# Top-k attention with an MLP behind it: 25 more items transposed by VectorE and DRAM, and q and k loaded in fewer DMAs

## The chip, the cores and the metric

The kernel runs on one core of one Trainium2 chip. The time is that of the device in microseconds (us), median of the runs of one kernel. A profile is one further execution with the hardware profiler. Engines are named as the profile names them: PE (TensorE), DVE (VectorE), ACT (ScalarE), POOL (GpSimd), SP (SyncE, which here only issues DMAs).

## What is computed

```python
scores = scale * np.matmul(q, k.transpose(0, 1, 3, 2))        # q, k, v: (8, 8, 576, 64) f32
kth = np.partition(scores, -32, axis=-1)[..., -32:-31]
scores = np.where(scores >= kth, scores, -1e9)
attn = np.exp(scores - max); attn = attn / (attn.sum(-1) + 1e-9)
x = np.matmul(attn, v)                                         # then (B, S, H*D) = 4608 x 512
g = gelu_exact(x @ w_in)                                       # w_in: 512 x 2048
out = g @ w_out                                                # w_out: 2048 x 512
```

All of it is float32. Each row of 576 scores keeps its 32 largest, and the softmax is taken over these.

## The kernel before

**Items.** Two heads make a pair (32 pairs in all, four to a batch). An item is one tile of 128 query rows of a pair, with both heads side by side: a tile of 128 x 1152 scores (`S_of`, tag "s", six buffers, L378). 576 rows are four tiles of 128 and 64 rows over; the 64 rows of two pairs form an item of their own. There are 18 items to a batch and 144 in all; `items` (L247 to L254) lists them so that tile t = 0 and 1 of pair 0 come first, then of pairs 1 to 3, then t = 2 and 3. In even batches the two items of the 64 rows stand last, in odd ones first. Thus an even item has t even, the odd one after it is the next tile of the same pair, and the two share one product with v.

**Slots.** The loop at L1154 runs over slots n. In slot n the scores of items ahead are made (L375; in even slots those of n+2 and n+3, the first in a PSUM tile of tag l1, which the MLP's first layer also uses, the second in tag pr), DVE does the top-k of item n (`top_k`, L457: four rounds of MAX8 and MATCH_REPLACE8 on each half), ACT does the selection and the exponentials of item n-1 (L512, L522), DVE takes the reciprocal of its sums at the end of the top-k (L504), POOL multiplies the item by it (`normalise`, L552). Item n-2 is transposed, so that keys lie on the partitions, and item n-3, if odd, is multiplied by v with the even one before it (`attend`, L696): ten products o of 128 x 64 and 128 x 256, and ACT copies o to xT (L720). The bank of o, of the transposes of the tails, of the last 64 keys' scores (L349) and of the first product of the second layer ("seven", L927) is one and the same, tag z.

**Two ways to transpose.** Most items go over PE: nine transposes against the identity (L619, L649) into PSUM, and two copies by ACT (L629, L664) into the tile `pt` (L597, L610; one buffer). Items for which `squared` (L558) holds, 48 even ones from item 28 on, go another way: in the middle of the top-k of slot i+2, ahead of its third round, DVE transposes squares of 32 x 32 (`square_p`, L565, one instruction over 128 x 1152), SP writes them to DRAM in four DMAs after that slot's top-k (`write_p`, L571), and at the start of slot i+3 reads them back into `pt` in four DMAs (`read_p`, L581), where the squares come to lie as a full transpose. An even item's `pt` is used in slot i+4.

**q and k.** From the second batch on, k and q of a pair are loaded in squares (L118 to L128) and turned by DVE (L282 to L288); the rows 512 to 575 of the two heads go to places of their own. Their loads are issued by SP when the pair before has been transposed (L314 to L317). v is loaded by tiles (L129 to L134).

**The MLP.** Its matmuls are cut in pieces (`l1_piece` L764, `trio_piece` L954, `seven_piece` L938), which `mlp` (L1077) puts between the attention's work so that each slot has its share: an even slot has seven pieces of the first layer, the odd slot after it the eighth, then "seven" and six of the second layer. Every engine, and SP's queue, works in the order in which this program issues.

Of the kernel before, what the change touches and what calls it, by code (L numbers as in the profile page):

```python
# [14 lines left out]
def kernel(  # L15
# [19 lines left out]
    nc = tc.nc  # L35
# [6 lines left out]
    P = 128  # L42
# [68 lines left out]
    def load(n, pair, queue=None, queue2=None):  # L111
        if pair >= n_pairs:
            return
        queue = queue or nc.sync
        queue2 = queue2 or queue
        b, h0 = pair // NP, 2 * (pair % NP)
        src = sources[n]
        if n != "v" and pair >= SQUARES:  # L118
            t = flat[n][0]
            for e in range(2):  # L120
                for d in range(2):
                    rows, cols = slice((2 * e + d) * SQ, (2 * e + d + 1) * SQ), slice(d * SQ, (d + 1) * SQ)
                    for at, lo, hi, by in ((0, 0, SM, queue), (SM + e * TL, SM, S, queue2)):
                        by.dma_start(
                            out=t[rows, at : at + hi - lo].rearrange("i (c j) -> i c j", j=SQ),
                            in_=src[b, h0 + e, lo:hi, cols].rearrange("(c i) j -> i c j", i=SQ),
                        )
            return  # L128
        t = raw_of(n, pair)  # L129
        for e in range(2):  # L130
            queue.dma_start(
                out=t[:, 0:NM, e, :], in_=src[b, h0 + e, 0:SM].rearrange("(t p) d -> p t d", p=P)
            )
            queue2.dma_start(out=t[e * TL : (e + 1) * TL, NM, e, :], in_=src[b, h0 + e, SM:S])  # L134

    load("k", 0, nc.scalar, nc.gpsimd)
    load("q", 0)
# [138 lines left out]
    def transpose_qk(pair, first=False):  # L276

        q_tail = SM + P
        done = set()

        def squares(c):
            rq, rk, kt = flat["q"][0], flat["k"][0], kt_of.get(pair)  # L282
            if c == 0:
                nc.vector.transpose(kt[:, 0:q_tail], rk)
            elif c == 1:
                nc.vector.transpose(kt[:, q_tail:], rq[:, SM:])
# [35 lines left out]

    S_of, stat_of = {}, {}

    def row(i, e):
        return S_of[i][:, e * S : (e + 1) * S]

# [16 lines left out]
    def last_keys(i, t_ps):  # L344
# [3 lines left out]
        if t < NM:  # L348
            nc.tensor.matmul(  # L349
                t_ps[:, 0:P], lhsT=q_of[pair][:, t * P : (t + 1) * P],  # L350
                rhs=kt_of[pair][:, SM : SM + P], start=True, stop=True,
            )
            if i == 0:
                return lambda: nc.vector.tensor_scalar(
                    s[:, SM : S + TL], t_ps[:, 0:P], scale, None, op0=ALU.mult
                )
            return lambda: nc.scalar.activation(
                s[:, SM : S + TL], t_ps[:, 0:P], func=AF.Copy, scale=scale
            )
        for r in range(2):  # L360
            kt = kt_of[pair + r]
            for e in range(2):
                nc.tensor.matmul(
                    t_ps[half(r, e), r * TL : (r + 1) * TL],
                    lhsT=kt[:, SM + P + e * TL : SM + P + (e + 1) * TL],
                    rhs=kt[:, SM + e * TL : SM + (e + 1) * TL],
                    start=True, stop=True,
                )
        return lambda: nc.scalar.activation(
# [4 lines left out]
    def scores(i, second=False):  # L374
# [7 lines left out]
        if t < NM:  # L382
            q_t, kt = q_of[pair][:, t * P : (t + 1) * P], kt_of[pair]
            for e in range(2):
                rows = slice(e * D, (e + 1) * D)
                nc.tensor.matmul(  # L386
                    s_ps[:, e], lhsT=q_t[rows, :], rhs=kt[rows, 0:SM], start=True, stop=True
                )
            if i == 0:

# [4 lines left out]
        else:  # L395

            for r in range(2):
                kt = kt_of[pair + r]
                for e in range(2):
                    rows = slice(e * D, (e + 1) * D)  # L400
                    nc.tensor.matmul(
                        s_ps[half(r, e), r, :], lhsT=kt[rows, SM + P + e * TL : SM + P + (e + 1) * TL],
                        rhs=kt[rows, 0:SM], start=True, stop=True,
                    )
            s2 = s.rearrange("p (r n) -> p r n", r=2)
            nc.scalar.activation(s2[:, :, 0:SM], s_ps, func=AF.Copy, scale=scale)
# [164 lines left out]
    def write_p(i):  # L571

        if squared(i):
# [3 lines left out]
            for a in range(P // SQ):  # L577
                rows = slice(a * SQ, (a + 1) * SQ)
                nc.sync.dma_start(out=d[:, :, rows], in_=s[rows])

    def read_p(i):  # L581

        if squared(i):
            d = turned.pop(i)
            for k in range(P // SQ):
                nc.sync.dma_start(
                    out=pt_now[0][k * SQ : (k + 1) * SQ, :, 0:P], in_=d[:, :, k, :]
                )

    def transposes(i):  # L590
# [3 lines left out]
        if squared(i):  # L594

            def keys_only(ahead):
                pt_now[0] = work.tile([P, 2 * NM + 1, 2 * P], f32, tag="pt", bufs=1, name="pt")  # L597
                if ahead is not None and ahead < N:
                    last_keys(ahead, bank("t_ps"))()

# [4 lines left out]
        def tails(ahead):  # L605
# [1 line left out]
            keys = last_keys(ahead, tp) if ahead is not None and ahead < N else None  # L607
            at = P
            if t % 2 == 0:
                pt_now[0] = work.tile([P, 2 * NM + 1, 2 * P], f32, tag="pt", bufs=1, name="pt")  # L610
            if diag is not None:
                for e in range(2):
                    nc.tensor.matmul(
# [540 lines left out]
    for n in range(ahead):  # L1154
# [165 lines left out]
```

## Time and profile before

| | |
|---|---|
| time, median of 3 runs (lowest to highest) | 1480.86 us (1480.14 to 1481.07) |
| the profiled execution | 1479.73 us, its span 1478.0 us |
| busy over the span: ACT, POOL | 74%, 77% |
| granted PE clock | 1.0 all through |
| DMA: moved, mean rate | 112.94 MB, 76 GB/s |

A span is from the first to the last instruction of the profiled execution. A row of a timeline has start and duration in us, engine, line, operation, tiles and shapes, how many instructions it merges, and in brackets the idle time ahead of them with what ended it. Matrix products and PE's float32 work come as two instructions each, transposes as one.

### The profile page before, as it was taken

What the parts mean: (1) busy time and instruction counts of PE and PEld (TensorE: products, weight loads), DVE (VectorE), ACT (ScalarE), POOL (GpSimd) and SP (SyncE); (2) the same over time, 40 slices, a digit from 0 to 9 for tenths busy, and PEclk for the clock granted to TensorE, in tenths of its full rate; (3) what the DMA queues carried; (4) which work ended last, traced back from release to release, by engine and by line L of the source; (5) the groups of instructions that cost most, each with busy time, mean ns of one, the idle gap of its engine ahead of it and who ended that gap; (6) DMA issues with size and microseconds to landing.
All of it is one profiled execution on the core that took longest, in us unless ns stands there. A gap on an engine that the chain in (4) does not pass through costs nothing. (4 is left out here: it accounts for less than half of the span.)

```text
span 1478.0 us, 27006 instructions
## 1 busy us (share of the span) xinstructions
PE 1461.6 (99%) x8817; PEld 1147.9 (78%) x8817; DVE 1294.3 (88%) x3318; ACT 1099.9 (74%) x1942; POOL 1140.1 (77%) x1291
## 2 busy tenths in 40 slices
PE   8999999999999999999999999999999999999999
PEld 6876677877777777887777778787777777787787
DVE  8999899999999988999999987999999997998701
ACT  7999977877777687777777778777777777776620
POOL 6877567877898879877898978886788887987732
PEclk9999999999999999999999999999999999999999
DMA  7424310045435322345534331345453421233300
GB/s 198 143 86 124 84 48 1 24 88 101 95 73 93 66 58 52 65 95 108 105 83 81 69 61 47 66 93 99 97 103 73 89 55 41 61 61 72 70 15 15
DMA packets 477645, 112.94 MB, mean 76 GB/s; under 512 B 413216, under 2 KB 469056, under 8 KB 477504
## 3 DMA queue, kind: packets, MB, share of 16 engines
q1 hardware_dynamic: 476240, 110.78, 35.3%
q8 instruction: 70, 1.15, 0.3%
q14 instruction: 71, 0.58, 0.1%
q10 hardware_dynamic: 1200, 0.39, 0.1%
q0 software_dynamic: 64, 0.03, 0.0%
HBM read 73.39 MB, written 37.75 MB: 75 GB/s over the span
## 5 line engine op out<-in xcount | busy, mean ns | idle before, releaser
L773 PE MATMUL h_ps<-xT,w_in_sb 128*128 128x256 f32 (+1 forms) x2560 | 536.2, 361 | 0.1
L773 PEld LDWEIGHTS h_ps<-xT,w_in_sb 128*128 128x128 f32 x2560 | 436.5, 190 | 73.4 <-issue 25.2
L483 DVE MAX8 top<-lists 128x8 f32<-128x576 f32 (+1 forms) x792 | 476.4, 641 | 0.0
L486 DVE MATCH_REPLACE8 lists<-top,lists 128x288 f32<-128x288 f32 (+1 forms) x528 | 307.9, 589 | 0.0
L552 POOL TENSOR_TENSOR s<-s,rden 128x1152 f32<-128x1152 f32 x135 | 285.8, 2117 | 0.3 <-DVE rden L504 0.3
L529 ACT ACTIVATE s<-s,bias 128x576 f32<-128x576 f32 x288 | 225.4, 787 | 11.0 <-issue 0.4
L517 ACT ACTIVATE s<-s,neg 128x576 f32<-128x576 f32 x288 | 225.5, 793 | 1.7 <-POOL neg L497 1.6
L510 POOL TENSOR_SCALAR den<-den 128x2 f32<-128x2 f32 x144 | 31.4, 218 | 215.9 <-ACT s L529 210.2
L455 POOL TENSOR_TENSOR lists<-lists 128x576 int32<-128x576 int32 x132 | 186.2, 1410 | 4.0
L447 POOL TENSOR_TENSOR lists<-s 128x576 int32<-128x576 int32 x133 | 187.2, 1407 | 0.0
L715 PE MATMUL o<-pt,raw_v 128*64 128x256 f32 x1280 | 153.0, 384 | 1.8 <-ACT s L529 1.1
L715 PEld LDWEIGHTS o<-pt,raw_v 128*64 128x64 f32 x1280 | 87.8, 136 | 85.8 <-issue 37.2
L789 ACT ACTIVATE g<-h_ps 128x512 f32<-128x512 f32 x144 | 78.2, 594 | 100.6 <-PE h_ps L773 100.4
L929 PE MATMUL y_ps<-w_out_sb,sum 128*128 128x256 f32 x472 | 140.4, 379 | 0.0
L394 ACT ACTIVATE s<-s_ps 128x1024 f32<-128x1024 f32 x127 | 125.5, 1035 | 10.5 <-PE s_ps L386 10.3
L664 ACT COPY pt<-tp 128x1024 f32<-128x1024 f32 x85 | 86.6, 1019 | 62.2 <-PE tp L649 62.1
L386 PE MATMUL s_ps<-kt,qm 64*128 64x512 f32 x512 | 129.4, 618 | 0.8 <-ACT s L392 0.8
L504 DVE RECIPROCAL rden<-den 128x2 f32<-128x2 f32 x144 | 23.2, 161 | 108.6 <-POOL den L510 107.4
L486 DVE MATCH_REPLACE8 lists<-first,lists 128x288 f32<-128x288 f32 x264 | 114.3, 439 | 0.0
L929 PE MATMUL y_ps<-w_out_sb,g 128*128 128x256 f32 x480 | 113.4, 379 | 0.0
L483 DVE MAX8 first<-lists 128x8 f32<-128x288 f32 x268 | 106.6, 436 | 0.0
L929 PEld LDWEIGHTS y_ps<-w_out_sb,g 128*128 128x128 f32 x480 | 91.2, 190 | 12.4
(167 smaller groups left out, 2533.1 us busy)
## 6 DMA issues: line engine op xcount, KB each, us to landing
turned<-s SPq DMA_DIRECT2D x192, 144.0 KB, 3.5
pt<-turned SPq DMA_DIRECT2D x192, 144.0 KB, 3.2
raw_v<-in_v_dram SPq DMA_DIRECT2D x64, 128.0 KB, 2.4
out_dram<-y SPq DMA_DIRECT2D x30, 256.0 KB, 2.1
raw_q<-in_q_dram SPq DMA_DIRECT2D x112, 64.0 KB, 2.0
raw_k<-in_k_dram SPq DMA_DIRECT2D x112, 64.0 KB, 2.0
w_out_sb<-in_moe_w_in_dram SPq DMA_DIRECT2D x14, 511.8 KB, 4.8
w_out_sb<-in_moe_w_out_dram SPq DMA_DIRECT2D x10, 511.8 KB, 4.1
```

What stands on the lines that cost most here:

```text
L386: nc.tensor.matmul(s_ps[:, e], lhsT=q_t[rows, :], rhs=kt[rows, 0:SM], start=True, stop=True)
L394: nc.scalar.activation(spread(s, S + TL, SM), s_ps, func=AF.Copy, scale=scale)
L447: nc.gpsimd.tensor_tensor(t[:, :, 1].bitcast(i32), a.bitcast(i32), b.bitcast(i32), op=ALU.add)
L455: nc.gpsimd.tensor_tensor(into_of(i)[:, :, 1].bitcast(i32), both, top, op=ALU.subtract)
L483: nc.vector.max(x[:, e], src[:, e])
L486: nc.vector.match_replace(dst[:, e], x[:, e], src[:, e], LOWEST)
L517: nc.scalar.activation(s, s, func=AF.Prelu, bias=st["neg"][:, e : e + 1], scale=1.0, alpha=STEEP)
L529: nc.scalar.activation(s, s, func=AF.Exp, bias=st["bias"][:, e : e + 1], scale=1.0, accum_out=st["den"][:, e : e + 1],)
L552: nc.gpsimd.tensor_tensor(s, s, wide, op=ALU.mult)
L715: nc.tensor.matmul(o[e * D : (e + 1) * D, 0:n], lhsT=vt[:, j, e, :], rhs=pt[:, e * NJ + j if j < NM else NM, :], start=(j == 0), stop=(j = ...
L773: nc.tensor.matmul(h_tile(u)[:, i, :], lhsT=w_in_sb[:, ko, f * P : (f + 1) * P], rhs=xT[:, ko, c0 : c0 + n], start=(ko == 0), stop=(ko == ...
L929: nc.tensor.matmul(acc[names][:, k], lhsT=lhsT, rhs=rhs, start=(j == 0 and k == 0), stop=(j == FT // 2 - 1 and k == 1),)
```

## The change

`squared` now also holds for an odd item whose pair is even within its batch and which is followed by an item that goes by squares (or by an item of the 64 rows). These are 25: 29, 33, 37, 41, 45, 49; 57 to 85 in steps of 4; 93 to 121 in steps of 4; 129, 133 and 137. Their tile is transposed by DVE in slot i+2, written at its end and read at the start of slot i+3, into the odd half of `pt`; `later` holds for them, and their product with v (with the copy of o) is issued at the end of slot i+3 and not after its scores. `pt` is now allocated where the even half is read.

The loads of k and q in squares take all 576 rows of a head and half in one DMA, four DMAs in place of eight. Both heads' keys lie in one run of 576 columns, the second head's 64 columns further on; the 64 keys that are handled apart are the first ones of the first head and the last ones of the second, so the columns of the main keys are 64 to 575 and the matmul of the last keys reads two runs of 64 columns, 576 apart (`both_ends`). The rows of v of the first head are taken in the matching order, and q's tail is 64 columns wide instead of 128 for DVE's transpose. The corner of k's tile that has to be zero is set once in slot 5.

```diff
@@ load
-                    for at, lo, hi, by in ((0, 0, SM, queue), (SM + e * TL, SM, S, queue2)):
-                        by.dma_start(
-                            out=t[rows, at : at + hi - lo].rearrange("i (c j) -> i c j", j=SQ),
-                            in_=src[b, h0 + e, lo:hi, cols].rearrange("(c i) j -> i c j", i=SQ),
-                        )
+                    queue.dma_start(
+                        out=t[rows, at : at + S].rearrange("i (c j) -> i c j", j=SQ),
+                        in_=src[b, h0 + e, :, cols].rearrange("(c i) j -> i c j", i=SQ),
+                    )
...
+            end = TL if pair >= SQUARES and e == 0 else S
+            main = end % S
@@ squares
-                nc.vector.transpose(kt[:, q_tail:], rq[:, SM:])
+                nc.vector.transpose(kt[:, q_tail : q_tail + TL], rq[:, SM:S])
@@ last_keys
-                rhs=kt_of[pair][:, SM : SM + P], start=True, stop=True,
+                rhs=both_ends(pair), start=True, stop=True,
@@ squared
-        return SINGLE.stop - 2 < i < N - 2 and i % 2 == 0 and items[i][1] < NM and i % RINGS != 12
+        if not SINGLE.stop - 2 < i < N - 2 or items[i][1] == NM:
+            return False
+        if i % 2 == 0:
+            return i % RINGS != 12
+        return items[i][0] % 2 == 0 and (squared(i + 1) or items[i + 1][1] == NM)
+
+    def later(i):
+
+        return i % 2 == 1 and squared(i)
@@ read_p
             d = turned.pop(i)
+            if i % 2 == 0:
+                pt_now[0] = pt_tile()
             for k in range(P // SQ):
                 nc.sync.dma_start(
-                    out=pt_now[0][k * SQ : (k + 1) * SQ, :, 0:P], in_=d[:, :, k, :]
+                    out=pt_now[0][k * SQ : (k + 1) * SQ, :, i % 2 * P : (i % 2 + 1) * P], in_=d[:, :, k, :]
                 )
@@ the loop over slots
-        product = attend(n - 3)
+        product = not later(n - 3) and attend(n - 3)
...
         run_gelus()
         mlp(left[0])
         run_gelus()
+        if later(n - 3):
+            attend(n - 3)
+            copy_x()
         if n < N:
             top_k(n, lambda: inverse(n - 1), lambda: square_p(n - 2))
             write_p(n - 2)
@@ n == 5
+            nc.vector.memset(flat["k"][0][TL:, 0:TL], 0.0)
```

More of the change, by code (lines that the diff above doesn't have):

```diff
@@ L323, with main_keys, end_keys, both_ends @@
     S_of, stat_of = {}, {}
+    def main_keys(pair):
+        return slice(TL, TL + SM) if pair >= SQUARES else slice(0, SM)
+    def end_keys(pair, e):
+        at = e * (SM + TL) if pair >= SQUARES else SM + e * TL
+        return slice(at, at + TL)
+    def both_ends(pair):
+        kt = kt_of[pair]
+        return spread(kt, SM + TL, TL) if pair >= SQUARES else kt[:, SM : SM + P]
+    def end_rows(pair, e):
+        at = SM + P + (0 if pair >= SQUARES else e * TL)
+        return slice(at, at + TL)
     def row(i, e):
@@ L364, in last_keys @@
                     t_ps[half(r, e), r * TL : (r + 1) * TL],
-                    lhsT=kt[:, SM + P + e * TL : SM + P + (e + 1) * TL],
-                    rhs=kt[:, SM + e * TL : SM + (e + 1) * TL],
+                    lhsT=kt[:, end_rows(pair + r, e)], rhs=kt[:, end_keys(pair + r, e)],
                     start=True, stop=True,
@@ L386, in scores @@
                 nc.tensor.matmul(
-                    s_ps[:, e], lhsT=q_t[rows, :], rhs=kt[rows, 0:SM], start=True, stop=True
+                    s_ps[:, e], lhsT=q_t[rows, :], rhs=kt[rows, main_keys(pair)], start=True, stop=True
                 )
@@ L401, in scores @@
                     nc.tensor.matmul(
-                        s_ps[half(r, e), r, :], lhsT=kt[rows, SM + P + e * TL : SM + P + (e + 1) * TL],
-                        rhs=kt[rows, 0:SM], start=True, stop=True,
+                        s_ps[half(r, e), r, :], lhsT=kt[rows, end_rows(pair + r, e)],
+                        rhs=kt[rows, main_keys(pair + r)], start=True, stop=True,
                     )
@@ L579, in write_p, with pt_tile @@
                 nc.sync.dma_start(out=d[:, :, rows], in_=s[rows])
+    def pt_tile():
+        return work.tile([P, 2 * NM + 1, 2 * P], f32, tag="pt", bufs=1, name="pt")
     def read_p(i):
@@ L596, in keys_only @@
             def keys_only(ahead):
-                pt_now[0] = work.tile([P, 2 * NM + 1, 2 * P], f32, tag="pt", bufs=1, name="pt")
                 if ahead is not None and ahead < N:
@@ L609, in tails @@
             if t % 2 == 0:
-                pt_now[0] = work.tile([P, 2 * NM + 1, 2 * P], f32, tag="pt", bufs=1, name="pt")
+                pt_now[0] = pt_tile()
             if diag is not None:
```

5 lines of the change are left out of this document (3 added, 2 removed).

## The prediction

> **What bounds the kernel now.** I read the page first, then the waits, then the timeline of TensorE, ScalarE, VectorE and SyncE over a few slots in the middle.
>
> ```profile
> span 1478.0 us, 27006 instructions
> PE 1461.6 (99%) x8817; PEld 1147.9 (78%) x8817; DVE 1294.3 (88%) x3318; ACT 1099.9 (74%) x1942; POOL 1140.1 (77%) x1291
> ```
>
> ```profile
> DVE rden L504 <- POOL den L510: 107.4, 92, 9.7
> ```
>
> TensorE has next to no idle time, so it sets the pace. VectorE is close behind: nearly all of its idle time (107.4 us over 92 of the 144 items) is a wait at the reciprocal that ends each top-k, for the sum that ScalarE delivers. The two therefore run in step, and a part moved from one to the other counts twice. The profiled execution took 1479.73 us (span plus 1.7), 1.1 below the median of the runs, so I add what I work out to the median, 1480.86.
>
> The timeline of TensorE (start, duration, instruction, count) around the product of item 69, one of the 25, and the transposes of item 71, which is not:
>
> ```profile
> 700.74 1.99 PE L386 MATMUL s_ps<-kt,qm 64*128 64x512 f32 x8
> 702.66 2.38 PE L715 MATMUL o<-pt,raw_v 128*64 128x256 f32 x20
> 704.97 2.86 PE L773 MATMUL h_ps<-xT,w_in_sb 128*128 128x256 f32 x12
> 707.66 0.38 PE L349 MATMUL t_ps<-kt,qm 128*128 128x128 f32 x2
> 707.88 4.48 PE L773 MATMUL h_ps<-xT,w_in_sb 128*128 128x256 f32 x20
> 712.20 1.03 PE L927 MATMUL seven<-w_sum,g 128*128 128x256 f32 x4
> ...
> 715.87 0.27 PE L619 MATMUL tp_t<-ident,s 128*128 128x128 f32 x1
> 715.98 0.60 PE L929 MATMUL y_ps<-w_sum,sum 128*128 128x256 f32 x2
> ...
> 716.85 1.04 PE L649 MATMUL tp<-ident,s 128*128 128x128 f32 x8
> 717.72 0.60 PE L929 MATMUL y_ps<-w_sum,g 128*128 128x256 f32 x2
> ```
>
> The starts follow each other without a gap, so the distance to the next start is what an instruction costs the path: 2.31 us for the product (702.66 to 704.97), 0.86 for a first-layer piece (a fifth of 707.88 to 712.20), 0.98 for the transposes of an item (0.11 at L619, 0.87 at L649).
>
> **The change, part by part.** Transposes taken off TensorE: 25 x 0.98 = 24.5 us. ScalarE loses the copies L629 and L664 with them, which is no gain by itself.
>
> VectorE gets 25 transposes. What one costs, where the even items have theirs:
>
> ```profile
> 578.75 0.14 DVE L504 RECIPROCAL rden<-den 128x2 f32<-128x2 f32 x1
> ...
> 582.69 1.41 DVE L483 MAX8 top<-lists 128x8 f32<-128x576 f32 x2
> ...
> 587.00 0.17 DVE L504 RECIPROCAL rden<-den 128x2 f32<-128x2 f32 x1
> ...
> 590.92 1.36 DVE L569 STREAM_TRANSPOSE s<-s 128x1152 f32<-128x1152 f32 x1
> 592.21 1.37 DVE L483 MAX8 top<-lists 128x8 f32<-128x576 f32 x2
> ...
> 596.60 0.17 DVE L504 RECIPROCAL rden<-den 128x2 f32<-128x2 f32 x1 [0.24 <-POOL den L510]
> ```
>
> 1.29 us each (590.92 to 592.21), 32 in all, against 107.4 of idle time: it fits on the whole, with little to spare where the items lie. In a slot without a transpose the third round starts 3.94 us after the reciprocal before it (578.75 to 582.69): there item 57's would go.
>
> The product moves behind the seven first-layer pieces that its slot has. Before, it stood between the scores and these pieces. The scores' first tile has the tag l1, as h_ps has, and ScalarE empties it:
>
> ```profile
> 701.98 1.94 ACT L394 ACTIVATE s<-s_ps 128x1024 f32<-128x1024 f32 x2 [0.27 <-PE s_ps L386]
> ```
>
> The first of the two copies ends at 702.95, the scores on TensorE at 702.66. With the product gone from between, the first piece waits 0.3 us and a hand-over, 0.35, in the 22 of 25 slots with two score items. Behind the moved product the eighth piece (0.86 us) covers the copy of o before the bank z is needed again: nothing. By TensorE alone that leaves 24.5 - 7.7 = 16.8 us gained.
>
> **The new wait** is the round trip through DRAM. An even item has two slots for it; an odd one is transposed in one slot and multiplied in the next. The SyncE queue, and what its transfers take to land:
>
> ```profile
> 592.35 3.26 SPq L579 DMA_DIRECT2D turned<-s  x4
> 598.47 2.54 SPq L586 DMA_DIRECT2D pt<-turned  x4
> ```
>
> ```profile
> turned<-s SPq DMA_DIRECT2D x192, 144.0 KB, 3.5
> ```
>
> ```profile
> L586 SPq DMA_DIRECT2D pt<-turned x192: 567/604/1378, 308.6 to 1392.8; - x192
> DMA to landing us min/median/max: 2.7/3.2/4.5
> ```
>
> Writes start 1.43 after the transpose does (590.92 to 592.35). The reads can go 6.1 later, when the last write has landed. The last of the four reads goes 1.9 after the first (three issues of 0.63) and lands 3.2 after that: 6.1 + 1.9 + 3.2 = 11.2 us; by the least and the largest landing of a read (2.7 and 4.5) 10.7 and 12.5. For item 57: transpose at 582.69, landed at 582.69 + 1.43 + 11.2 = 595.3. For TensorE the slot of item 69 serves: scores, 0.35, then 6.37 for seven pieces with L349 (2.91 + 16/20 of 4.32), so the product is due 8.6 us after the scores began. The wait that falls out is 1 to 4 us, and what stands behind it on TensorE is everything.
>
> Whether this is paid once or each time is seen from the loop it closes, which holds every fourth slot. Its other legs:
>
> ```profile
> 692.51 0.14 DVE L504 RECIPROCAL rden<-den 128x2 f32<-128x2 f32 x1
> 712.11 0.14 DVE L504 RECIPROCAL rden<-den 128x2 f32<-128x2 f32 x1
> 720.85 0.17 DVE L504 RECIPROCAL rden<-den 128x2 f32<-128x2 f32 x1 [0.62 <-POOL den L510]
> 730.85 0.14 DVE L504 RECIPROCAL rden<-den 128x2 f32<-128x2 f32 x1
> ```
>
> ```profile
> 717.92 1.01 ACT L664 COPY pt<-tp 128x1024 f32<-128x1024 f32 x1 [0.95 <-PE tp L649]
> ```
>
> Transpose of item j to the product: 1.43 + 11.2 = 12.6. Product and eighth piece: 2.31 + 0.86 = 3.2. From there (712.20) TensorE does item j+2's transposes, ScalarE waits for them (L664) and does the second half's softmax, and VectorE's reciprocal waits for that: to 720.85, 8.65. Then VectorE's next slot, 9.36 (587.00 to 596.60 less 0.24), and 3.94 to the transpose of item j+4. Sum: 37.7 us. Added on its legs are k's and q's transposes, 0.75 and 0.8, by
>
> ```profile
> L284 DVE STREAM_TRANSPOSE kt<-raw_k 128x640 f32<-128x640 f32 x28 | 23.3, 832 | 0.0
> L286 DVE STREAM_TRANSPOSE kt<-raw_q 128x128 f32<-128x128 f32 x28 | 8.2, 292 | 0.8 <-DMA raw_q<-in_q_dram 0.8
> ```
>
> and the SyncE queue, where the loads of k or q stand ahead of the write:
>
> ```profile
> 699.13 4.08 SPq L124 DMA_DIRECT2D raw_k<-in_k_dram  x8
> ...
> 736.23 4.08 SPq L124 DMA_DIRECT2D raw_q<-in_q_dram  x8
> ```
>
> With four DMAs these take half, 2.04 (an estimate from the rows: equal issues; the ends are nothing gained, 4.08, and 2.04). Item 69's transpose would end at 692.51 + 3.94 + 0.75 + 1.29 = 698.5, its write starts behind k's loads at 701.2: 2.6 late. Item 73's: 736.9 against 738.3, 1.3 late.
>
> From item 57 to item 85 there are seven loops: 7 x 37.7 = 263.9, plus 0 (nothing is loaded or transposed on its legs), 0.8 (q's), 0.7 (k's), 4.1 (the loop from item 69: both transposes, 1.5, and the late write, 2.6), 1.3 (item 73's late write), 1.5 (both) and 0.4 (both, but its even slot, item 84, has no transpose of its own) = 8.8, so 272.7. In the trace the same two places lie 267.2 apart (582.69 to 849.85):
>
> ```profile
> 849.85 1.41 DVE L483 MAX8 top<-lists 128x8 f32<-128x576 f32 x2
> ```
>
> +5.5, or 0.8 a loop. The 25 items (29 to 49, 57 to 85, 93 to 121, 129 to 137) have 5 + 7 + 7 + 2 = 21 loops: +16.5. The last item of the first three groups has no loop behind it, only the wait:
>
> ```profile
> 854.71 2.38 PE L715 MATMUL o<-pt,raw_v 128*64 128x256 f32 x20
> 857.01 2.86 PE L773 MATMUL h_ps<-xT,w_in_sb 128*128 128x256 f32 x12
> 863.83 1.09 PE L401 MATMUL s_ps<-kt 64*64 64x512 f32 x8
> ```
>
> Item 85 lands at 849.85 + 12.6 = 862.5; TensorE is there at 854.71 - 0.98 + 6.82 (857.01 to 863.83) = 860.5, a wait of 2.0 against 0.98 saved: +1 each, +3. **Sum: +19.5, so 1500 us.** By the two ends of the trip, 0.5 less or 1.3 more in each of 21 loops, it would be 1490 or 1527.
>
> Costed at nothing. The score tiles rotate over six buffers, so ScalarE's second L394 (item j+6) must now wait until item j's write has landed, 3 to 5 us. Behind it queue the two softmax halves; VectorE's own work to the next reciprocal, 14 us after the transpose, covers them with some 0.3 to 2 us to spare, and if that goes it costs 1 us a time, 25 in all. q's narrower tail transpose saves VectorE at most 28 x 0.15; the split moving operand of L349 has the same columns, and between nothing and half of its 0.22 us a time lies open. The one memset is under 0.2 us. v's loads keep their count.
>
> On the trip the Trainium skill speaks for the change: DMA: Bandwidth & Descriptors, Anatomy of one DMA, gives a fixed 2.0 us per DMA plus bytes over 436 GB/s, most of it the write receipt. By that (stated for GpSimd's queue) a 144 KB transfer lands in an estimated 2.3 us, and the trip is 2.55 + 2.3 + 1.9 + 2.3 = 9.1. The trace says 3.5 and 3.2, and it decides. VectorE: DVE Perf Modes, Rules for kernel authors, speaks against it: a 128x128 transpose belongs on TensorE where PSUM will do.
>
> **The rivals.**
> 1. *The trip fits: faster.* A loop is 39.0 us with its additions and the cycle of the trace 38.2. Were the trip 0.8 shorter (10.4) nothing would be lost, and from 9.7 on TensorE would set the pace and keep its 16.8 us: 1464, or up to 1476 where VectorE, now some 98% busy in these slots, takes part back. For it: the least landing of a read is 2.7, not 3.2. Against it: the 6.1 from first write to first read is the wait itself. Chance 0.17.
> 2. *A draw*, 1478 to 1484: TensorE's gain goes into waits of the same size. Chance 0.08.
> 3. *The trip grows, or ScalarE's wait for the score buffer shows:* SyncE has three round trips in four slots in place of two, and each late write moves what is queued behind it. 1 us more a loop: 1525, up to 1540. Chance 0.18.
>
> **How the numbers follow.** The forecast, slower by the loop, 1484 to 1515, has 0.57. The range leaves out half of the first rival and the end of the third: 1470 to 1528. A measurement tells 0.2% (3 us) from no change. Faster 0.17, within 0.08, slower 0.57 + 0.18 = 0.75.
>
> **What would show it.** Right: TensorE, now without idle time, waits 25 to 50 us in all ahead of L715, with the transfer pt<-turned as releaser, in the slots of the 25 items and longest for items like 69 and 73; ScalarE waits ahead of L394 for a DMA; 25 more of L569 at 1.36 us; x696 of L649 becomes x496. Wrong: L715 of these items starts right behind L773; or VectorE has no idle time left at L504, so that it is the bound and not the trip; or the reads come much less or more than 6 us after the writes.

## The result, and the profile after

The changed kernel takes 1542.79 us (median of four runs, 1541.72 to 1545.34), the kernel before 1480.78 on the same chip (1480.14 to 1481.07): a ratio of 1.0423, interval 1.041 to 1.0436. It is slower by 62.0 us, where 19.5 had been predicted (1500, range 1470 to 1528): the direction was right, the size three times too small. The profiled execution took 1545.34 us, its span is 1543.6. The lines below are those of the changed file: MAX8 is now L504, the reciprocal L525, DVE's square transpose L598, the write L608, the read L620, the product with v L748, the first layer L806, the copy of o L753, ACT's score copy L415.

The page of the changed kernel, its span and the busy time of the engines:

```profile
span 1543.6 us, 26596 instructions
PE 1463.0 (95%) x8592; PEld 1138.2 (74%) x8592; DVE 1323.7 (86%) x3344; ACT 1071.1 (69%) x1892; POOL 1141.8 (74%) x1291
```

TensorE has 225 instructions less and yet is busy 1.4 us longer than before, in a span 65.6 us longer: it lost time, and it also ran slower. The groups by shape say where (line, engine, instruction, count, then busy us and mean ns of one, then idle time ahead and what ended it):

```profile
L748 PE MATMUL o<-pt,raw_v 128*64 128x256 f32 x1280 | 170.7, 416 | 59.7 <-DMA pt<-turned 33.0 <-DMA raw_q<-in_q_dram 15.2 <-DMA turned<-s 9.1
L598 DVE STREAM_TRANSPOSE s<-s 128x1152 f32<-128x1152 f32 x73 | 99.7, 1366 | 0.0
L682 PE MATMUL tp<-ident,s 128*128 128x128 f32 x496 | 64.4, 273 | 0.0
```

The counts of L598 and L682 are as predicted: 25 more square transposes on DVE, 200 transposes less on PE. New is 59.7 us of idle time ahead of the product with v. Every releaser named there is a transfer on SyncE's queue; q's loads share it with the reads into `pt`, and whichever record came last is named. Item by item, 57.6 of it stands ahead of the 25 moved products, and 2.1 ahead of the others. And the product's mean is 416 ns, where the kernel with only the new loads (below) has 384.

The timeline of TensorE in the changed kernel around the product of item 73 (start, us, instruction, count, idle time and its releaser):

```profile
769.70 2.86 PE L806 MATMUL h_ps<-xT,w_in_sb 128*128 128x256 f32 x12 [0.43 <-ACT s L415]
...
772.61 3.62 PE L806 MATMUL h_ps<-xT,w_in_sb 128*128 128x256 f32 x16
780.64 4.07 PE L748 MATMUL o<-pt,raw_v 128*64 128x256 f32 x20 [4.42 <-DMA turned<-s]
784.64 1.13 PE L806 MATMUL h_ps<-xT,w_in_sb 128*128 128x256 f32 x4
```

Three costs are to be seen in it: 0.43 us ahead of the first piece, 4.42 ahead of the product, and a product that takes 4.00 (780.64 to 784.64) where the same twenty instructions took 2.31. For the third, busy time by stretches: length, PE, PEld, DVE, ACT, POOL (with instructions), granted clock, DMA share, GB/s:

```profile
780.60:784.70 4.10, 4.05 (x21) 2.48 (x21) 3.46 (x12) 0.00 (x0) 3.94 (x6) 0.58 0.59 90
784.70:795.00 10.30, 10.30 (x54) 7.92 (x55) 5.38 (x13) 9.51 (x16) 7.27 (x11) 1.00 0.35 111
```

The clock granted during that product is 0.58, and 1.00 behind it. Ten of the 25 products (33, 37, 45, 49, 69, 73, 81, 105, 109, 117) take 3.6 to 4.5 us, 17.8 us in all above 2.31.

SyncE's queue for the same item, which DVE transposes at

```profile
765.41 1.37 DVE L598 STREAM_TRANSPOSE s<-s 128x1152 f32<-128x1152 f32 x1
```

is this:

```profile
763.58 3.13 SPq L620 DMA_DIRECT2D pt<-turned  x4
766.80 2.17 SPq L124 DMA_DIRECT2D raw_q<-in_q_dram  x4
769.08 3.44 SPq L608 DMA_DIRECT2D turned<-s  x4
775.07 2.54 SPq L620 DMA_DIRECT2D pt<-turned  x4
```

The transposed tile is ready at 766.78. SyncE has just finished the read of the even item before and issues q's loads; the write starts at 769.08, 2.30 late. The first read follows 5.99 after the first write, the product 5.57 after the first read. Such late writes, of 1.47 to 2.79 us, occur at nine items (33, 37, 45, 69, 73, 81, 105, 109, 117), and 0.56 at item 129; the others start within 0.1.

What waits in the changed kernel besides TensorE (engine, what it issues, what ended the wait: total, times, longest):

```profile
ACT xT L753 <- PE o L748: 150.5, 57, 7.9
DVE rden L525 <- POOL den L531: 144.7, 78, 9.8
...
ACT s L415 <- DMA turned<-s: 50.7, 14, 6.2
```

VectorE's idle time at the reciprocal grew from 107.4 to 144.7 us although VectorE got more to do: it is not the engine that the others wait for over the whole span. ScalarE's wait for the score buffer is there as foreseen, 50.7 us.

SyncE's own waits ahead of the reads, in the changed kernel and then in the kernel before (where the read is L586):

```profile
SPq L620 <- DMA turned<-s: 159.6, 99, 3.6
```

```profile
SPq L586 <- DMA turned<-s: 95.2, 64, 4.0
```

### The profile page after: what moved, and what is told of

Same layout as the page of the kernel before. It is cut to its first block, busy times and chain, and to the rows that moved or that the text cites. A ratio compares the mean times of both kernels' runs of the same rounds, so it can differ in the third digit from the quotient of the medians.

```text
span 1543.6 us, 26596 instructions
## 1 busy us (share of the span) xinstructions
PE 1463.0 (95%) x8592; PEld 1138.2 (74%) x8592; DVE 1323.7 (86%) x3344; ACT 1071.1 (69%) x1892; POOL 1141.8 (74%) x1291
## 2 busy tenths in 40 slices
DMA packets 621259, 142.39 MB, mean 92 GB/s; under 512 B 528032, under 2 KB 612672, under 8 KB 621120
## 5 line engine op out<-in xcount | busy, mean ns | idle before, releaser
L806 PE MATMUL h_ps<-xT,w_in_sb 128*128 128x256 f32 (+1 forms) x2560 | 543.8, 363 | 7.4 <-ACT s L415 7.4
L806 PEld LDWEIGHTS h_ps<-xT,w_in_sb 128*128 128x128 f32 x2560 | 436.4, 191 | 101.8 <-issue 28.7
L504 DVE MAX8 top<-lists 128x8 f32<-128x576 f32 (+1 forms) x792 | 475.6, 640 | 0.1
L748 PE MATMUL o<-pt,raw_v 128*64 128x256 f32 x1280 | 170.7, 416 | 59.7 <-DMA pt<-turned 33.0
L748 PEld LDWEIGHTS o<-pt,raw_v 128*64 128x64 f32 x1280 | 101.8, 148 | 135.5 <-issue 86.5
L415 ACT ACTIVATE s<-s_ps 128x1024 f32<-128x1024 f32 x127 | 127.8, 1034 | 95.6 <-DMA turned<-s 50.7
L525 DVE RECIPROCAL rden<-den 128x2 f32<-128x2 f32 x144 | 22.7, 157 | 145.0 <-POOL den L531 144.7
L518 POOL TENSOR_SCALAR neg<-top 128x2 f32<-128x2 f32 x144 | 66.6, 463 | 90.6 <-DVE rden L525 78.4
L753 ACT COPY xT<-o 128x256 f32<-128x256 f32 x64 | 24.7, 385 | 150.5 <-PE o L748 150.5
L504 DVE MAX8 first<-lists 128x8 f32<-128x288 f32 x268 | 106.7, 437 | 0.0
```

Of the source, the lines that this page charges most:

```text
L415: nc.scalar.activation(spread(s, S + TL, SM), s_ps, func=AF.Copy, scale=scale)
L504: nc.vector.max(x[:, e], src[:, e])
L748: nc.tensor.matmul(o[e * D : (e + 1) * D, 0:n], lhsT=vt[:, j, e, :], rhs=pt[:, e * NJ + j if j < NM else NM, :], start=(j == 0), stop=(j = ...
L806: nc.tensor.matmul(h_tile(u)[:, i, :], lhsT=w_in_sb[:, ko, f * P : (f + 1) * P], rhs=xT[:, ko, c0 : c0 + n], start=(ko == 0), stop=(ko == ...
```

## The experiments

Theory: the round trip of the odd items is longer than the one slot that it has, and TensorE waits it out, the loop closing through ScalarE and VectorE. Rivals: VectorE has no room for 25 transposes; the transfers hold something else up (ScalarE's score buffer, or the queue); the moved product costs by its place; the clock. The odd branch of `squared` and the condition of `later` can be set apart, so that each part runs by itself. Ratios are to the kernel before on the same chip, whose median is 1480.4 to 1480.9 throughout.

**The parts that don't touch DRAM.** loads_only keeps the new loads and drops the 25 items:

```diff
-        return items[i][0] % 2 == 0 and (squared(i + 1) or items[i + 1][1] == NM)
+        return False
```

> The kernel after without the 25 odd items: they go over TensorE as before, and only the four loads of 576 rows (with the new order of the keys) are left of the change. Theory (the 62 us come from TensorE's wait for the round trip of odd items, and from the lower clock that follows such a wait): 1476 to 1482 us, as before, for the loads were off the path. Rival that the new loads cost (72 KB land later than 64, the split operand of L371 is slower): 1495 or more.

1480.03 us, 0.9998 (0.9988 to 1.0007): the fewer loads are worth nothing either way, as costed.

late_only does the same, but lets `later` hold for the 25 items, so that their product moves and nothing else does.

> The new loads and, for the same 25 items, the product with v at the slot's end, but their transposes stay on TensorE: no round trip for them. Theory: the move costs the wait of the first-layer piece for the tile l1, 0.35 us in 22 slots, so about 8 us: 1483 to 1493. Rival that the place of the product is what costs (ScalarE waited 150 us in all for o in the kernel after, against 64): 1515 or more.

1493.02, 1.0086 (1.0071 to 1.0101): the place costs 12.4 us, where 7.7 had been worked out; that is the very end of the range expected. Its first-layer rows, then loads_only's row for the larger shape (and its product with v, for the mean of 384 above):

```profile
L809 PE MATMUL h_ps<-xT,w_in_sb 128*128 128x256 f32 x2048 | 480.4, 383 | 7.4 <-ACT s L415 7.4
L809 PE MATMUL h_ps<-xT,w_in_sb 128*128 128x128 f32 x512 | 61.7, 277 | 1.6 <-ACT s L415 1.6
```

```profile
L806 PE MATMUL h_ps<-xT,w_in_sb 128*128 128x256 f32 x2048 | 475.3, 383 | 0.0
...
L748 PE MATMUL o<-pt,raw_v 128*64 128x256 f32 x1280 | 152.9, 384 | 1.9 <-ACT s L550 1.2 <-ACT pt L687 0.4 <-ACT pt L697 0.2
```

The waits for the tag l1 are 9.0 us in 22 places, and the larger shape of the first layer is busy another 5.1 us at the same mean per instruction. Busy time counts overlapping instructions once, so this reads as less overlap behind the wait, a slower restart; no run isolated it. Together that is 14.1, enough for the 12.4; what took 1.7 back was not pursued.

**The transfers without the product's wait.** no_wait leaves everything in place, but the moved products read the even half of `pt` twice (so the odd items' weights are left out of them), and wait for no odd read:

```diff
-                        rhs=pt[:, e * NJ + j if j < NM else NM, :],
+                        rhs=spread(pt[:, e * NJ + j if j < NM else NM, 0:P], 0, P) if later(i)
+                        else pt[:, e * NJ + j if j < NM else NM, :],
```

> The kernel after, with every transfer and every VectorE transpose, but the product of the 25 items takes the even item's half of pt for both halves, so that it doesn't wait for the odd item's read (this leaves out the odd items' weights in those products). Theory: the wait and the clock loss go, TensorE keeps what it saved, as far as VectorE lets it: 1462 to 1482. Rival that VectorE's 32 us more, or ScalarE's wait for the score buffer, or the traffic itself sets the time: 1520 to 1543.

1501.74, 1.0143 (1.0128 to 1.0158): a miss. Of the 62 us 41 go with the wait, as the theory says; but 21 stay, in a kernel that has 24.5 us less of transposes on TensorE. So something else costs too. The next kernels take it apart, all with these products, each leaving out one thing more: no_wait_no_dve has no transpose by DVE for the 25 items (the data is written untransposed), no_trip has neither transpose nor write nor read.

```diff
-        if squared(i):
+        if squared(i) and not later(i):
```

This is the edit in `square_p`; in no_trip `read_p` has it too, and `write_p` only gives the odd tile's buffer back.

> The kernel no_wait (product of the 25 items on the even half twice) and without VectorE's transpose of the 25 items, which are written to DRAM as they are (so their squares aren't turned, and nothing reads them). Theory now: of the 21 us that no_wait still lost, VectorE's 1.29 us in slots without idle time is the larger part: 1468 to 1485. Rival that ScalarE's wait for the score buffer, or the traffic, is it: 1497 to 1503.

> The kernel no_wait_no_dve without the 25 items' transfers too: they are neither turned, nor written, nor read (their product takes the even item's half twice). What is left is TensorE's saving of 24.5 us and the product's later place, which cost 12.4 by itself: theory, 1480.4 - 24.5 + 12.4 = 1468, so 1465 to 1474, and the 11 to 23 us above that in no_wait_no_dve belong to the transfers, by way of the score buffer or the traffic. Rival that leaving TensorE's transposes out gains nothing, since ScalarE or VectorE hold the pace: 1483 to 1493.

no_wait_no_dve 1491.53, 1.0076 (1.0063 to 1.009), missed; no_trip 1469.24, 0.9921 (0.9907 to 0.9936), as expected. From late_only to no_trip the transposes leave TensorE and nothing comes: -24.1, the 24.5 of the prediction. From no_trip to no_wait_no_dve come the transfers alone: +22.9. From there to no_wait come DVE's transposes: +10.0. And from no_wait to the changed kernel comes the product's own wait: +40.9.

**Why transfers whose data nobody uses cost over 20 us.** In no_wait_no_dve ScalarE waits for the score buffer, and even items' products wait too:

```profile
ACT s L415 <- DMA turned<-s: 43.2, 16, 5.4
...
PE o L748 <- DMA pt<-turned: 15.7, 9, 3.0
```

Which of the two is it? other_source is no_wait_no_dve with a tile of weights written to DRAM in place of the scores, so that the score buffer comes free without a transfer; other_source_dve is the same with DVE's transposes.

```diff
-            s = S_of.pop(i).rearrange("p (x j) -> p x j", j=SQ)
+            s = S_of.pop(i)
+            if later(i):
+                s = w_in_sb[:, 0, 0 : 2 * S]
+            s = s.rearrange("p (x j) -> p x j", j=SQ)
```

> The kernel no_wait_no_dve, but the 25 items' writes to DRAM take their data from w_in_sb, not from the score tile: the same transfers, and the score tile is free when it has been normalised. Theory that ScalarE's L415 waits for the score buffer (43 us of waits in no_wait_no_dve): as no_trip, within 4 us. Rival that the traffic or SyncE's queue costs: 1486 to 1493.

> The kernel other_source with VectorE's 25 transposes again (of score tiles that nobody reads then). If VectorE's part is its own, it is above other_source by what no_wait was above no_wait_no_dve, 10 us: 8 to 13. Rival that the two waits hide each other, so that VectorE's part is larger where the score buffer is free: 15 or more.

1491.4, 1.0075 (1.0058 to 1.0092), and 1499.13, 1.0126 (1.011 to 1.0142). ScalarE's 43.2 us are gone from the waits of other_source, and the time is the same as that of no_wait_no_dve: the score buffer was not it. With VectorE's transposes the free buffer gives 18.2 us above the kernel before in place of 21.1 (other_source_dve, no_wait), a difference that the intervals don't tell from none. VectorE's part is 7.7 us here, just under the 8 to 13 expected and the 10.0 found above. What stays in other_source is the wait of the even items' products, and SyncE's own waits (here L623 is the read):

```profile
PE o L751 <- DMA pt<-turned: 18.5, 10, 3.3
```

```profile
SPq L623 <- DMA turned<-s: 91.9, 63, 3.9
...
SPq L623 <- DMA turned<-w_in_sb: 64.7, 36, 3.2
```

The read of an odd item may be issued only when its write has landed. SyncE stands still for that, 64.7 us in all, and what is queued behind it, the even item's write and then its read, starts later. no_landing_wait keeps all transfers of other_source, but lets the odd reads fetch from q, so that they wait for no write:

```diff
+            if later(i):
+                d = q.rearrange("b h s d -> (b h s d)")[0 : SQ * (NJ + NM) * P // SQ * P]
+                d = d.rearrange("(i c k n) -> i c k n", c=NJ + NM, k=P // SQ, n=P)
```

> The kernel other_source, but the odd items' reads take as many bytes from q in DRAM, so that SyncE doesn't wait for the odd items' writes to land ahead of them (what they read is not used). Theory that SyncE's queue costs by these waits (64.7 us in 36 of them) and so delays the even items' reads, for which other products then waited 20 us: 1470 to 1479. Rival that the issues themselves (200 more, some 130 us on SyncE) or the traffic cost: 1486 to 1493.

1470.89, 0.9939 (0.9924 to 0.9954). Its reads are L626:

```profile
SPq L626 <- DMA turned<-s: 96.1, 65, 4.3
```

The 64.7 us of standing still are gone, and with them 20.5 us of the time. 25 more round trips' worth of traffic costs 1.7 us against no_trip. other_source and no_landing_wait move the same 142.39 MB. So it is neither bandwidth nor the buffer: it is the queue that stands.

**The clock.** filled puts twelve products with the identity, into the tag of o, ahead of the moved product of nine items, so that TensorE isn't idle there. filled_short puts six, ahead of eleven items (with 57 and 129).

```diff
+            if n - 3 in (33, 37, 45, 69, 73, 81, 105, 109, 117):
+                warm = bank("warm")
+                for _ in range(12):
+                    nc.tensor.matmul(warm[:, 0:P], lhsT=ident, rhs=ident, start=True, stop=True)
```

> The kernel after with 12 matmuls of 128x128 on the identity (some 2.8 us) ahead of the product in the nine items whose wait was over 3 us, so that TensorE is busy in most of that wait. Theory with the clock: in the kernel after the product of ten items took 3.6 to 4.5 us in place of 2.31, 18 us in all, since the granted clock fell to 0.58 there; kept busy it doesn't fall: 1522 to 1532. Rival: these products are slow for another reason (data that lands piece by piece): 1540 to 1546.

> The kernel after with 6 matmuls on the identity (1.5 us) ahead of the product in eleven items with long waits; in the kernel filled 12 of them ended after the data had landed and took part of the gain back. Theory with the clock: no product takes over 2.4 us, and the 17.8 us of slow products turn into time: 1522 to 1531. Rival that the slow product is no loss, because ScalarE or VectorE is as late: 1537 to 1543.

filled: 1538.37, 1.0395 (1.0375 to 1.0415), a miss; filled_short: 1530.1, 1.033 (1.0313 to 1.0347), as expected. Item 69 in filled:

```profile
731.03 2.94 PE L1288 MATMUL warm<-ident 128*128 128x128 f32 x24 [0.80 <-ACT s L379]
734.03 2.38 PE L748 MATMUL o<-pt,raw_v 128*64 128x256 f32 x20
```

All nine products run in 2.31 us again, but the fill first waits for its bank (0.4 to 2.2 us) and then takes longer than the transfer; 57 and 129, without a fill, now wait 3.9 and 3.6 us and are slow (4.47). With six products (twelve instructions), item 69:

```profile
724.45 1.60 PE L1288 MATMUL warm<-ident 128*128 128x128 f32 x12 [0.68 <-ACT s L379]
727.63 2.38 PE L748 MATMUL o<-pt,raw_v 128*64 128x256 f32 x20 [1.57 <-DMA pt<-turned]
```

The wait is split, and the product is fast. Three are slow in this kernel (93, 117, 121: 4.00, 4.46, 3.67), against the expectation that none would be: 93 and 121 have no fill, and the fill of 117 waits 2.04 us for its bank, so that TensorE is idle all the same. Filling the wait thus gives back 12.7 of the 62 us, and slow products fall from 17.8 us to 5.2.

**The late write.** held_loads issues the loads of q and k behind the write of the slot instead of ahead of it, except in the last pairs of odd batches:

```diff
+            put = issue if pair >= SQUARES and not (pair // NP % 2 and pair % NP > 1) else (lambda f: f())
...
-                load("q", pair + ahead)
+                put(lambda: load("q", pair + ahead))
...
-                load("k", pair + ahead)
+                put(lambda: load("k", pair + ahead))
```

> The kernel after, but k's and q's loads go behind the writes of the slot and not ahead of them, except in the last pairs of odd batches, whose loads are soon needed. Theory (the late write lengthens the round trip, and a wait over 3 us lowers the clock too): the write starts at once after its transpose in the nine items in which it was 1.5 to 2.8 us late, which saves these and the slow products, about 9 x (2 + 1.9) = 35: 1503 to 1520. Rival that the order on SyncE is covered by something else that waits as long (the score buffer): 1535 to 1543.

1529.18, 1.0329 (1.0307 to 1.035): 13.6 less, not the 23 to 40 expected. Its queue where k and then q are loaded:

```profile
757.64 3.39 SPq L609 DMA_DIRECT2D turned<-s  x4
761.08 3.13 SPq L124 DMA_DIRECT2D raw_q<-in_q_dram  x4
764.37 2.54 SPq L621 DMA_DIRECT2D pt<-turned  x4
```

The write is no longer behind q's loads, but now the loads stand between write and read, and the read comes 6.73 after the write instead of 5.99. The products of the 25 items still wait 43.5 us and are slow by 5.5, and the other products now wait 8.2. Against the changed kernel's profile all products together wait 8.1 us less, and slow products cost 12.2 less: most of what this order gains is the clock (the profiled execution, at 1523.87, was the fastest of the four).

**One slot more for the trip.** slot_after puts the moved product and the read of the next even item into the following slot, behind four pieces of its MLP work:

```diff
-        read_p(n - 3)
+        if not later(n - 4):
+            read_p(n - 3)
...
+        if later(n - 4):
+            held[0] = True
+            attend(n - 4)
+            copy_x()
+            read_p(n - 3)
+            flush()
...
-        if later(n - 3):
-            attend(n - 3)
-            copy_x()
```

> The kernel after, but the product of the 25 items is issued in the slot after, behind its first four MLP pieces (some 3.6 us later), and the read of the even item behind it. Theory: the round trip has the time that it needs, 57.6 us of waits and 17.7 of slow products go but for a few: about what the kernel without the wait had, 1497 to 1510. Rival that moving the product later only moves the wait on (ScalarE's copy of o and the even item's read then come late): 1520 to 1545.

> slot_after with k's and q's loads behind the writes as in held_loads: the correct version with both mends. Theory: the late writes are all that is left of TensorE's waits, and the score buffer is free some 2 us earlier in nine items: 1496 to 1504. Rival that the trip no longer matters in slot_after: 1503 to 1507. Neither expects it to beat the kernel before.

1504.94, 1.0169 (1.0153 to 1.0185); with the held loads as well 1502.28, 1.0145 (1.013 to 1.016). Both are as expected. In slot_after no moved product is slow any more, and the wait of the 25 falls to 8.8 us. Now the other products wait, 15.3 us, mostly for the even read that stands behind. This fits the 20 us of the queue, which the longer wait had covered; no run of this order isolated it.

**Fewer items, and a mended order.** six_items keeps only 61, 65, 97, 101, 133 and 137, whose waits were short.

> The kernel after with six odd items instead of 25: 61, 65, 97, 101, 133 and 137, in whose slots VectorE had 1.4 to 2.3 us of idle time and whose read landed within 0.7 us of the product's turn. Theory: TensorE saves 6 x (0.98 - 0.35) = 3.8 us and VectorE's part is covered: 1474 to 1480, the version that may beat the kernel before. Rival that each odd item loses wherever it lies: 1486 or more.

1484.04, 1.0023 (1.0013 to 1.0032), a miss: even six cost 3.7 us, 0.6 each. mended combines slot_after and held_loads and issues the odd read behind the next item's write, so that SyncE has something to issue while the first write lands, and the even read behind the moved product; mended_six does it for the six. Both also put the last keys' matmul and the transposes of the slot ahead of its first-layer pieces, so these runs don't tell one of the changes from another.

```diff
-        read_p(n - 3)
+        if not later(n - 4) and not later(n - 3):
+            read_p(n - 3)
...
             write_p(n - 2)
+            if later(n - 3):
+                read_p(n - 3)
```

> A correct version with the mends that the runs point to: the odd item's read goes behind the next item's write, so that SyncE needn't stand still for its landing; the product goes into the slot after, behind four MLP pieces; k's and q's loads go behind the writes; and the last keys' matmul goes ahead of the first-layer pieces, to cover part of their wait for l1. Theory: no_landing_wait (1471) with VectorE's 8 to 10 us, less some 4 of the l1 wait: 1474 to 1486, about as before. Rival that the read, issued half a slot later, is late again and the wait returns: 1495 or more.

> The same for the six items 61, 65, 97, 101, 133 and 137, where VectorE had idle time. Theory: TensorE keeps 6 x 0.7 = 4 us, VectorE's part is covered: 1475 to 1480. Rival that an odd item loses in any case (six_items was 3.7 us above the kernel before): 1482 to 1486.

1659.4, 1.1208 (1.1192 to 1.1223), and 1524.09, 1.0292 (1.0278 to 1.0306): both far off the hope, and the slowest of all for their number of items. In mended_six the queue and the product of item 61:

```profile
633.87 2.73 SPq L609 DMA_DIRECT2D turned<-s  x3
636.76 3.00 SPq L621 DMA_DIRECT2D pt<-turned  x4
```

```profile
643.21 4.34 PE L749 MATMUL o<-pt,raw_v 128*64 128x256 f32 x20 [5.02 <-DMA raw_k<-in_k_dram]
```

The read needn't wait for a landing any more, but it begins only once the next write has been issued: its last DMA is issued at 639.76, and TensorE had reached the product at 638.19. In mended the waits of the 25 sum to 133.0 us and slow products to 44.8. Among the orders that were run none gives the trip its time and the queue its freedom together, and no kernel that does the 25 transposes this way beats the kernel before.

## Why the prediction was right in direction and wrong in size

In sum, by the differences above (each time taken against its own kernel before, and good to about 2 us; the order in which the parts are added is a choice, since they cover each other): place of the product +12.4, transposes off TensorE -24.1, transfers +22.9, DVE's transposes +10.0, the product's own wait +40.9, of which some 13 is the clock; together +62.1 against 62.0. From product to product, the 21 loops of the changed kernel take 860.3 us, where the same products lie 801.2 apart in the kernel before: 59 of the 62 us are in the loops, where the prediction had put 16.5.

**Right.** The 24.5 us saved on TensorE (24.1). The trip as the price: without the product's wait, the landing wait and VectorE's transposes nothing is left of the loss (no_landing_wait). Its legs: 6.1 us from write to read (5.9 to 6.2 in most items, 6.5 to 7.2 in seven) and 5.1 from read to product (5.2 to 6.3 measured). The total of waits ahead of the product, forecast at 25 to 50, came to 57.6, somewhat above. Nothing for the loads (0.9998), and nothing that the runs can tell for the score buffer, although ScalarE does wait for it.

**Wrong: the loop, put at 0.8 us more than before.** The seven loops from item 57 to item 85 were put at 37.7, 38.5, 38.4, 41.8, 39.0, 39.2 and 38.1, sum 272.7; by the ends of DVE's transposes they are 38.1, 38.6, 39.7, 42.7, 42.0, 39.4 and 44.1, 284.5. The path was the predicted one, and the size was off: (284.5 - 267.2) / 7 = 2.5 us a loop instead of 0.8, which over 21 loops is 52 instead of 16.5. Of the 11.8 us that the seven loops have too many, 5.2 are slow products (items 69, 73 and 81), 2.7 a trip from write to product longer than 11.2 (at most 12.36, at item 65), 1.9 writes that are later than reckoned, and 2.0 were not taken apart. So the largest piece is a term that the sum did not have.

**Wrong: the late write "only at items 69 and 73".** It was reckoned at 2.6 and 1.3 us, and came to 1.65 and 2.30; item 81, reckoned at nothing, has 2.00. In the three groups of items the same three places are late, which makes the nine. The trace of before held the third: there too k's loads come right behind a read in the slot that item 81's transpose would go to.

```profile
806.70 0.14 DVE L504 RECIPROCAL rden<-den 128x2 f32<-128x2 f32 x1
```

```profile
808.90 2.54 SPq L586 DMA_DIRECT2D pt<-turned  x4
811.48 4.58 SPq L124 DMA_DIRECT2D raw_k<-in_k_dram  x8
```

By the prediction's own rule the transpose would end at 806.70 + 3.94 + 0.75 + 1.29 = 812.7, and half of these loads at 813.8: 1.1 late. The late writes cost twice: all nine of their products are slow as well (16.2 of the 17.8 us), and only one other is.

**Wrong: TensorE at full speed after a wait.** The sum used 2.31 for each product. The granted clock drops in the ten products named above, and 13 to 18 us were missing from the sum. The Trainium skill has this rule, in TensorE: Matmul & The Clock Gate, Part 1 (The HAM clock gate): after an idle window of some 3.4 us the array is clocked at half rate, and the window runs free. The traces agree on the rate and the steps: the granted clock is 0.50 or 1.00, and changes only at steps of 3.41 us. They differ on the idle window, which need not be idle throughout. Four such steps of the changed kernel, two at item 49 and two at item 129 (columns as above):

```profile
532.00:535.41 3.41, 1.32 (x7) 0.81 (x5) 3.41 (x7) 0.00 (x0) 3.33 (x6) 1.00 0.81 183
535.41:538.83 3.42, 3.20 (x16) 2.13 (x18) 3.42 (x8) 0.00 (x0) 2.76 (x5) 0.50 0.87 134
```

```profile
1351.21:1354.62 3.41, 1.83 (x9) 1.27 (x7) 3.41 (x8) 3.29 (x7) 3.33 (x4) 1.00 0.61 170
1354.62:1358.03 3.41, 1.91 (x18) 1.59 (x20) 3.02 (x7) 0.45 (x2) 3.25 (x7) 1.00 0.90 136
```

Item 49 waited only 2.31 us, but 2.09 of it lay in one step, 0.61 of it idle: the next step is at half clock. Item 129 waited 3.08, split over two steps that were idle for 0.46 and 0.44, and stayed fast. All ten drops of the changed kernel follow a step that was idle for 0.60 or more, and a step of 0.55 or less was not followed by one; over all profiled executions here, from 300 us to 4 us before the end, the bounds are 0.60 and 0.59 (one drop ahead of that, in held_loads, followed 0.48). So the length of a wait doesn't tell it alone: it counts where the wait lies in the steps. The prediction itself forecast waits and would have had to reckon with this.

**Wrong: VectorE "fits on the whole", at no cost.** It costs 10.0 us (no_wait against no_wait_no_dve; 7.7 by other_source_dve against other_source). The 107.4 us of idle time were a total. Where it counts, a slot that has none, the row comes later. In the changed kernel the slot with item 57's transpose, between two reciprocals:

```profile
602.49 0.15 DVE L525 RECIPROCAL rden<-den 128x2 f32<-128x2 f32 x1
...
606.43 1.37 DVE L598 STREAM_TRANSPOSE s<-s 128x1152 f32<-128x1152 f32 x1
...
611.79 0.15 DVE L525 RECIPROCAL rden<-den 128x2 f32<-128x2 f32 x1
```

9.30 us, where the same slot took 8.25 before; neither reciprocal waited. The idle time of later slots doesn't give it back: what VectorE waits for there, ScalarE's sum, hangs on VectorE's own threshold of the slot before, so the wait moves with the row. That last step is read from the program and the rows' lateness; no run isolated it.

**Wrong: the transfers at nothing but the trip itself.** SyncE's queue was counted for the odd items' own write and read, not for what stands behind it. The read's landing wait delays the even items' transfers, 20.5 us once the longer wait is taken away (no_landing_wait against other_source). The Trainium skill gives the reason why it can't be left out, in DMA: Bandwidth & Descriptors, Two DMAs through the same engine are not ordered: a transfer that reads what an earlier one wrote has to wait for the earlier one's completion, though both are on one queue. The 99 waits ahead of L620 are that wait; the kernel before had 64 of them.

**Too low: the place.** 0.35 us in 22 places was 7.7; it is 12.4, with waits of 9.0 and the busy time behind them.

**The third rival** named the right cause in half a sentence (three round trips in four slots, each late write moves what is behind it) and was priced at 1 us more a loop, 1525 to 1540. It was 1.7 more (2.5 in place of 0.8), and even the upper end was passed. The first rival, that the trip fits, would have needed a trip of at most 10.4 us from write to product; the shortest among the 25 was 11.07 (item 133), and item 73's was 11.56 (769.08 to 780.64), behind a write 2.30 late.

**Open.** Whether another queue for the odd trip would free SyncE was not tried. How the costs cover each other is known only in the one order in which the parts were added.

## What to carry to other kernels

Where a dependent transfer is put on a shared queue, count what stands behind its landing wait as well as the trip itself; here that was 20.5 us, a third of the loss, and it came up only when the larger wait was taken away. Idle time of an engine in a ring of dependencies is room only in the slot where it lies; look at the slot that gets the work, not at the total. And a wait on TensorE of 2 to 6 us can have a second price behind it: look at the granted clock of the stretch that follows.

## What the runs showed of the hardware beyond what was expected

The granted clock is 0.58 over one product (0.50 over those of items 37, 45, 81 and 117) and back at 1.00 right behind it, so that the mean over the span (0.984) hides where it costs. It went to half after a step of 3.41 us in which TensorE was idle for six tenths, and not only after an idle one. Six short products with the identity within the wait were enough to keep the product at 2.31 us in item 69, but not in item 117, where they came late. Four DMAs of 144 KB each keep SyncE's queue for 2.5 to 3.4 us in the rows shown, and 25 more tiles of four such writes and four reads cost 1.7 us of time when the reads don't wait for the writes to land.
